# Twelve pairs of weight buffers shifted in 32-byte steps against the activations they are multiplied with

## The chip, the core and the metric

The kernel runs on one core of a Trainium2 chip. The metric is the device time of one execution in microseconds (us). The core's engines are called PE (TensorE's matrix multiplies), PEld (its weight loads, which run beside the multiplies), DVE (VectorE), ACT (ScalarE), POOL (GpSimd) and SP (SyncE, which issues the DMAs here).

## The reference

Linear attention with a feature map, then two multilayer perceptrons on its output:

```python
def phi(x):                                   # x: (4, 8, 576, 64), w_phi: (64, 128)
    proj = np.einsum('bhsd,df->bhsf', x, w_phi)
    proj = proj - np.max(np.abs(proj), axis=-1, keepdims=True)
    return np.concatenate([np.exp(proj), np.exp(-proj)], axis=-1)
q_p, k_p = phi(q), phi(k)
kv = np.einsum('bhsf,bhsd->bhfd', k_p, v);  z = np.sum(k_p, axis=2)
num = np.einsum('bhsf,bhfd->bhsd', q_p, kv)
den = np.einsum('bhsf,bhf->bhs', q_p, z)[..., None] + 1e-06
x = (num / den) as (2304 tokens, 512)
h = x @ w_in1;  x = (h * np.cos(h)) @ w_out1                            # 512 -> 2048 -> 512
h = x @ w_in2;  out = (max(h, 0) + alpha * min(h, 0)) @ w_out2          # 512 -> 2048 -> 512
```

The four weight matrices come in 8-byte floats; the kernel takes them as pairs of 32-bit words and decodes them on the chip.

## The kernel before

**Attention first.** Eight groups of four heads are worked off in chunks of tokens: projections (`pj`, line 455), the sums over keys (`kv`, line 496), transposes (`tp`, line 536) and the numerators (`nm`, line 580). The normalised result is written as two tiles, `xh` and `xl`, each 128 partitions x 4 x 2304 of type float32r. `xh` is the value rounded to float32r, `xl` is what is left over.

**Then the two perceptrons.** Every operand of these products is such a high and low pair, and `mm3` (line 160) makes each product of three multiplies: high by high, high by low, low by high. The hidden features are cut into 16 tiles of 128 per layer, the tokens into groups of 512, 512, 512, 512 and 256. A step is one feature tile for one token group: `hidden` makes four products, 12 multiplies into a PSUM tile `ph`, with the weights `wih`, `wil` stationary and `xh`, `xl` moving. `turns`, `gate` and `activate` make the activation and its pair `gh`, `gl` on ACT, DVE and POOL, some steps ahead. `output` makes again 12 multiplies (6 for the 256-token group in the second layer, where the tokens are the rows) into PSUM tiles `po`: in layer 1 with `woh`, `wol` stationary and `gh`, `gl` moving, in layer 2 the other way round. The Python code fixes the order of every engine's instructions; there is no planner behind it.

**The weight buffers.** `w_tile` (line 90) gives each decoded weight tile a buffer of 128 partitions x 512 float32r values, 2048 bytes in a partition. There are six slots (`WSLOTS`), each with a high and a low buffer for `w_in` (`wih0`, `wil0`, ...) and for `w_out` (`woh0`, `wol0`, ...), so twelve pairs. Slots 0 and 1 lie in `wpool`, slots 2 to 5 in `wpool2`, which is opened where the attention's buffers were. `w_instructions` (line 95) decodes a tile in ten instructions on ACT, DVE and POOL; `fetch_w` (line 138) starts its DMA.

**Where things lie.** In the built program, `xh`, `xl`, all five buffers each of `gh` and `gl`, and all 24 weight buffers start at a byte address that leaves 352 when it is divided by 512. (A tile of 128 bytes, `edge`, at the far end of the memory is used by nothing and shifts `gh` and `gl` there.) Every piece of 128 weight columns and every 512-token piece of x begins a multiple of 512 bytes further, so that in the perceptrons the stationary operand that is being loaded and the moving operand that is being streamed always lie at distance 0 modulo 512. In the attention's numerators they don't: the stationary tiles `kvh`, `kvl` start at 480, 32, 96 and 160 modulo 512, are read in pieces of 66 columns (264 bytes) at offsets that are multiples of 264, and the moving tiles `qp0h`, `qp0l`, `qp1h`, `qp1l` are read from 224 and 480.

Of the kernel before, what the change touches and what calls it, by code (L numbers as in the profile page):

```python
# [10 lines left out]
F32 = mybir.dt.float32  # L11
# [10 lines left out]
P = 128  # L22
# [6 lines left out]
def feature_map_attention_two_mlps(  # L29
# [52 lines left out]
    w_t = {}  # L82
    w_pools, w_temps = [wpool], [wtmp]
    staged, decoding = [], []

    def split(hi, lo, src, lo_engine):
        nc.scalar.copy(hi, src)  # L87
        lo_engine.tensor_tensor(out=lo, in0=src, in1=hi.bitcast(F32), op=ALU.subtract)  # L88

    def w_tile(slot, nm):  # L90
        s = slot % WSLOTS
        pool = w_pools[0 if s < WSLOTS_A else 1]
        return pool.tile([P, DM], F32R, tag=f"{nm}{s}", name=f"{nm}{s}")

    def w_instructions(spare=True):
# [15 lines left out]
        def to_hi():  # L111
            hl.extend(w_tile(layer * NFT + ft, f"w{'io'[which]}{x}") for x in "hl")
            w_t[layer, which, ft] = tuple(
                z.rearrange("p (k f) -> p k f", k=KD) if which == 0 else z for z in hl
            )
            copy(hl[0], tf)
# [683 lines left out]
```

## Time and profile before

| | |
|---|---|
| time, median of 2 runs | 987.65 us (987.52 to 987.78) |
| time of the profiled execution | 987.77 us |
| its span, from the first to the last instruction | 986.0 us |
| mean granted TensorE clock | 0.999 of 2.4 GHz |
| PE busy | 978.1 us (99%), 5145 multiplies |
| PEld busy | 838.0 us (85%) |
| DVE, ACT, POOL busy | 688.5, 493.9, 606.5 us |

The multiplies overlap one another in the records (one of 512 columns is shown as 390 ns long), so a busy PE says only that it never ran dry. How fast it goes is read from the distance between the starts of two multiplies that follow each other; below this is called a step.

### The profile page before, as it was taken

To read this page: it belongs to the slowest core of one execution; us is meant where nothing else is said; L and a number is where in the kernel's file an instruction comes from. 1 tells how busy PE (TensorE), PEld (TensorE's weight loads), DVE (VectorE), ACT (ScalarE), POOL (GpSimd) and SP (SyncE) were. 2 spreads that over 40 slices of the span, in tenths; PEclk is the share of its full clock that TensorE was granted. 3 is DMA by queue.
4 is the path that set the end of the run, shared out by engine and by line. 5 is a ranking of instruction groups with operands and counts; after the bars stand their busy time and mean duration, and the time that the engine had idled before them with its cause. 6 is when DMAs were issued, how large, how long until landed. Compare 5 with 4: busy or idle time off the path is not lost.

```text
span 986.0 us, 13997 instructions
## 1 busy us (share of the span) xinstructions
PE 978.1 (99%) x5145; PEld 838.0 (85%) x5145; DVE 688.5 (70%) x976; ACT 493.9 (50%) x967; POOL 606.5 (62%) x498
## 2 busy tenths in 40 slices
PE   8999999999999999999999999999999999999998
PEld 7999999888888888888888888888888888888886
DVE  6878687677987577747774788588748874885343
ACT  5888788867666467546755654132213221322110
POOL 3577777856666457535756789567636763676221
PEclk9999999999999999999999999999999999999999
DMA  6454544211121112101110112011101110110112
GB/s 164 113 140 126 142 114 115 66 52 51 57 65 44 43 43 65 44 22 43 64 44 22 44 43 65 22 43 65 43 22 44 65 43 23 43 64 1 43 59 91
DMA packets 64580, 60.63 MB, mean 61 GB/s; under 512 B 28928, under 2 KB 54656, under 8 KB 64512
## 3 DMA queue, kind: packets, MB, share of 16 engines
q1 hardware_dynamic: 64512, 59.75, 20.5%
q8 instruction: 40, 0.66, 0.3%
q14 instruction: 28, 0.23, 0.1%
HBM read 52.50 MB, written 4.79 MB: 58 GB/s over the span
## 4 chain that ended last, share of the span: by engine, by line
PE 94%; ACT 2%; DVE 1%; issue 1%; DMA 1%; POOL 1%; SPq 0%; POOLq 0%; ACTq 0%
PE po L165 39%; PE ph L165 38%; PE pj L455 6%; PE kv L496 5%; PE nm L580 5%; PE tp L536 2%; DMA acc<-in_q_dram 0%; DMA dn<-acc 0%; ACT acc L555 0%; DVE r L192 0%; DVE wt L127 0%; ACT acc L593 0%; ACT r L195 0%; ACT r L184 0%; ACT r L196 0%
## 5 line engine op out<-in xcount | busy, mean ns | idle before, releaser
L88 POOL TENSOR_TENSOR gl<-r,gh 128x512 fp32r<-128x512 f32 (+1 forms) x160 | 204.2, 1277 | 294.7 <-ACT gh L87 289.7
L87 ACT CAST gh<-r 128x512 fp32r<-128x512 f32 (+1 forms) x160 | 92.1, 576 | 382.5 <-DVE r L211 261.8
L165 PE MATMUL ph<-xl,wih 128*128 128x512 f32 (+1 forms) x640 | 235.7, 368 | 0.3 <-POOL xl L624 0.3
L165 PE MATMUL ph<-xh,wih 128*128 128x512 f32 (+1 forms) x640 | 235.5, 368 | 0.0
L165 PE MATMUL ph<-xh,wil 128*128 128x512 f32 (+1 forms) x640 | 235.4, 368 | 0.0
L245 DVE TENSOR_TENSOR acc<-po,acc 128x512 f32<-128x512 f32 (+1 forms) x134 | 86.1, 658 | 96.9 <-PE po L165 96.9
L165 PEld LDWEIGHTS ph<-xl,wih 128*128 128x128 f32 x640 | 120.6, 188 | 21.1 <-POOL xl L624 0.6
L165 PEld LDWEIGHTS ph<-xh,wih 128*128 128x128 f32 x640 | 120.6, 188 | 20.7
L165 PEld LDWEIGHTS ph<-xh,wil 128*128 128x128 f32 x640 | 120.5, 188 | 20.1
L165 PE MATMUL po<-gh,wol 128*128 128x512 f32 (+1 forms) x320 | 117.8, 368 | 0.2 <-POOL wol L135 0.2
L165 PE MATMUL po<-gl,woh 128*128 128x512 f32 (+1 forms) x320 | 117.9, 368 | 0.0
L165 PE MATMUL po<-gh,woh 128*128 128x512 f32 (+1 forms) x320 | 117.9, 368 | 0.0
L165 PE MATMUL po<-woh,gh 128*128 128x512 f32 x288 | 112.4, 390 | 0.0
L165 PE MATMUL po<-wol,gh 128*128 128x512 f32 x288 | 112.3, 390 | 0.0
L165 PE MATMUL po<-woh,gl 128*128 128x512 f32 x288 | 112.1, 389 | 0.1
L124 DVE SCALAR_TENSOR_TENSOR wt<-ws,we 128x512 int32<-128x512 int32 x64 | 98.4, 1537 | 2.4
L198 DVE TENSOR_SCALAR r<-ph,al 128x512 f32<-128x512 f32 (+1 forms) x80 | 55.3, 691 | 55.8 <-PE ph L165 35.6
L209 DVE TENSOR_TENSOR r<-ph,r 128x512 f32<-128x512 f32 (+1 forms) x80 | 50.5, 631 | 48.5 <-ACT r L196 48.3
L133 POOL TENSOR_TENSOR wu<-wu,we 128x512 f32<-128x512 f32 x64 | 82.9, 1295 | 1.3 <-ACT wu L130 1.3
L571 POOL TENSOR_TENSOR qp1l<-acc,qp1h 128x512 fp32r<-128x512 f32 (+1 forms) x64 | 59.2, 951 | 26.6 <-ACT qp1h L569 26.6
L496 PEld LDWEIGHTS kv<-vm,kp 128*128 128x128 f32 x512 | 72.5, 191 | 2.6 <-ACT qp1h L569 0.4
L496 PE MATMUL kv<-vm,kp 128*128 128x66 f32 x512 | 72.5, 255 | 0.1
(81 smaller groups left out, 1877.5 us busy)
## 6 DMA issues: line engine op xcount, KB each, us to landing
ws<-in_moe_w_in_dram SPq DMA_DIRECT2D x32, 512.0 KB, 3.7
ws<-in_moe_w_out_dram SPq DMA_DIRECT2D x32, 512.0 KB, 3.5
acc<-dr SPq DMA_DIRECT2D x32, 144.0 KB, 3.1
out_dram<-acc SPq DMA_DIRECT2D x18, 256.0 KB, 2.0
vm<-in_v_dram SPq DMA_DIRECT2D x16, 256.0 KB, 3.7
kin<-in_k_dram SPq DMA_DIRECT2D x28, 128.0 KB, 2.9
qin<-in_q_dram SPq DMA_DIRECT2D x28, 128.0 KB, 2.9
acc<-acc SPq DMA_DIRECT2D x16, 144.0 KB, 2.3
```

Of the source, the lines that this page charges most:

```text
L87: nc.scalar.copy(hi, src)
L88: lo_engine.tensor_tensor(out=lo, in0=src, in1=hi.bitcast(F32), op=ALU.subtract)
L124: lambda: stt(out=t, in0=w1, scalar=-0x40000000, in1=e, op0=ALU.bitwise_and, op1=ALU.bitwise_or),
L133: lambda: tt(out=u, in0=u, in1=ef, op=ALU.mult),
L165: nc.tensor.matmul(ps, lhsT=l, rhs=r, start=(first and m == 0), stop=(last and m == n - 1))
L198: nc.vector.tensor_scalar(out=r, in0=ph, scalar1=0.0, scalar2=al[:, ft:ft + 1], op0=ALU.min, op1=ALU.mult)
L209: nc.vector.tensor_tensor(out=r, in0=ph, in1=r, op=ALU.mult)
L245: nc.vector.tensor_tensor(out=a, in0=po, in1=a, op=ALU.add)
L455: nc.tensor.matmul(pj[:, a].rearrange("p j f -> p (j f)"), lhsT=x[:, a * P:(a + 1) * P], rhs=w2.rearrange("p j f -> p (j f)"), start=True, ...
L496: nc.tensor.matmul(ps[:, :, y, :] if pr is None else ps[:, pr, y, :], lhsT=e[:, s, 2 * a + y, :], rhs=vt[:, y] if pr is None else vm[:, pr ...
L571: nc.gpsimd.tensor_tensor(out=dl, in0=et, in1=dh.bitcast(F32), op=ALU.subtract)
L580: nc.tensor.matmul(nm, lhsT=l[:, s, pr, y * VW:(y + 1) * VW], rhs=r[:, s, y, :], start=(s == 0 and m == 0), stop=(s == 1 and m == 2),)
```

## The change

The first time that the high buffer of a pair is asked for, an unused tile of 128 partitions x 8 float32 values (32 bytes in a partition) is taken from the same pool just ahead of it:

```diff
+    skewed = set()
 ...
     def w_tile(slot, nm):
         s = slot % WSLOTS
         pool = w_pools[0 if s < WSLOTS_A else 1]
+        if nm[2] == "h" and (nm, s) not in skewed:
+            skewed.add((nm, s))
+            pool.tile([P, 8], F32, tag=f"{nm}{s}skew", name=f"skew{s}")
         return pool.tile([P, DM], F32R, tag=f"{nm}{s}", name=f"{nm}{s}")
```

In the built program the pairs then start at these distances behind x (and behind `gh`, `gl`, which stay where they were), modulo 512; high and low buffer of a pair have the same one:

| pair | slot 0 | slot 1 | slot 2 | slot 3 | slot 4 | slot 5 |
|---|---|---|---|---|---|---|
| `wih`, `wil` | 32 | 64 | 160 | 192 | 288 | 320 |
| `woh`, `wol` | 96 | 128 | 224 | 256 | 352 | 384 |

What is allocated behind them on the same side moves too: the accumulators `acc` and all of the attention's left-hand tiles (`qin`, `kvh`, `kvl`, `qp0h` and so on) by 128 bytes, the second set of decoding temporaries by 384. The tiles on the right (`kin`, `kp`, `vm`, `gh`, `gl`, `r`) do not move. The instructions of every engine, their order and their waits are the same as before, row by row; only line numbers and addresses differ.

## Rows read from the trace of the kernel before

**Rows 1.** The page's parts 1 and 4: busy engines, and the chain by line.

```profile
PE 978.1 (99%) x5145; PEld 838.0 (85%) x5145; DVE 688.5 (70%) x976; ACT 493.9 (50%) x967; POOL 606.5 (62%) x498
...
PE po L165 39%; PE ph L165 38%; PE pj L455 6%; PE kv L496 5%; PE nm L580 5%; PE tp L536 2%; DMA acc<-in_q_dram 0%; DMA dn<-acc 0%; ACT acc L555 0%; DVE r L192 0%; DVE wt L127 0%; ACT acc L593 0%; ACT r L195 0%; ACT r L184 0%; ACT r L196 0%
```

**Rows 2.** Whom PE waited for: total us, times, longest us.

```profile
PE tp L432 <- DVE half_pi L434: 1.5, 1, 1.5
PE pj L455 <- DMA acc<-in_q_dram: 1.2, 1, 1.2
PE tp L536 <- ACT qp0h L569: 0.4, 1, 0.4
PE ph L165 <- POOL xl L624: 0.3, 1, 0.3
PE po L165 <- POOL wol L135: 0.2, 1, 0.2
```

**Rows 3.** PE's groups by shape: count | busy us, mean ns | idle before.

```profile
L165 PE MATMUL ph<-xh,wih 128*128 128x512 f32 x512 | 199.5, 390 | 0.0
...
L165 PE MATMUL po<-woh,gh 128*128 128x512 f32 x288 | 112.4, 390 | 0.0
...
L165 PE MATMUL po<-gh,woh 128*128 128x512 f32 x256 | 99.8, 390 | 0.0
...
L165 PE MATMUL ph<-xh,wih 128*128 128x256 f32 x128 | 36.0, 282 | 0.0
...
L165 PE MATMUL po<-gh,woh 128*128 128x256 f32 x64 | 18.0, 282 | 0.0
```

**Rows 4.** Chain of work, 215 to 240 us: start us, us, what.

```profile
222.84 2.72 PE po L165 x12
225.56 2.72 PE ph L165 x12
```

**Rows 5.** Chain of work, 519 to 530 us: a 256-token group in layer 1.

```profile
523.53 1.43 PE ph L165 x12
524.96 2.75 PE po L165 x12
```

**Rows 6.** PE's timeline behind those 256-column multiplies: start us, shown length us.

```profile
524.80 0.40 PE L165 MATMUL po<-gh,woh 128*128 128x512 f32 x1
525.03 0.40 PE L165 MATMUL po<-gl,woh 128*128 128x512 f32 x1
525.27 0.39 PE L165 MATMUL po<-gh,wol 128*128 128x512 f32 x1
525.50 0.40 PE L165 MATMUL po<-gh,woh 128*128 128x512 f32 x1
525.73 0.39 PE L165 MATMUL po<-gl,woh 128*128 128x512 f32 x1
525.96 0.39 PE L165 MATMUL po<-gh,wol 128*128 128x512 f32 x1
```

**Rows 7.** PE's timeline at 39 us: numerators, `kvh` from 480 modulo 512.

```profile
39.55 0.31 PE L580 MATMUL nm<-qp1h,kvl 128*66 128x320 f32 x1
...
40.42 0.31 PE L580 MATMUL nm<-qp1h,kvl 128*66 128x320 f32 x1
```

**Rows 8.** PE's timeline at 62 us: the same, `kvh` from 32 modulo 512.

```profile
62.52 0.31 PE L580 MATMUL nm<-qp1h,kvl 128*66 128x320 f32 x1
...
63.41 0.32 PE L580 MATMUL nm<-qp1h,kvl 128*66 128x320 f32 x1
```

**Rows 9.** PE's timeline at 191 us: the last group's numerators, then layer 1.

```profile
191.45 0.28 PE L580 MATMUL nm<-qp0h,kvh 128*66 128x256 f32 x1
...
192.75 0.28 PE L580 MATMUL nm<-qp0h,kvl 128*66 128x256 f32 x1
192.87 0.40 PE L165 MATMUL ph<-xh,wih 128*128 128x512 f32 x1
```

**Rows 10.** PE's timeline at 151 us: float32 projections, two passes a multiply.

```profile
151.29 1.03 PE L455 MATMUL pj<-w,kin 128*128 128x256 f32 x4
152.15 0.59 PE L455 MATMUL pj<-w,qin 128*128 128x256 f32 x2
```

**Rows 11.** PEld's groups by shape: count | busy us, mean ns | idle before.

```profile
L165 PEld LDWEIGHTS ph<-xh,wih 128*128 128x128 f32 x640 | 120.6, 188 | 20.7
...
L580 PEld LDWEIGHTS nm<-qp1h,kvh 128*66 128x66 f32 x64 | 8.8, 138 | 0.7
```

## The prediction

> **What bounds the kernel now.** I read the page's busy engines and its chain by line first, then PE's waits, then PE's multiplies by shape, and last the chain and PE's timeline inside the perceptrons. The first two say that nothing but TensorE counts: PE is busy for 978.1 of 986.0 us, the chain lies on it for 94% by the sum of its lines, 77% in `ph` and `po` alone, and all of PE's shown waits together are 3.6 us [rows 1, 2]. DVE at 70%, POOL at 62% and ACT at 50% are cover enough: in the whole run PE waited once for a decoded weight, 0.2 us [rows 1, 2]. So the change can only count through the steps of the multiplies themselves, and through those that read a weight buffer.
>
> There are 3 x (512 + 288 + 256) = 3168 of them with 512 moving columns and 3 x (128 + 64) = 576 with 256 [rows 3]; each of these rows stands for three of one count, for high by high, high by low and low by high. Twelve of the large ones take 2.72 us, so a step is 226.7 ns; twelve of the small ones take 1.43 us, 119.2 ns [rows 4, 5]. The difference, 107.5 ns for 256 columns, is 0.42 ns a column, which is 2.4 GHz, the clock granted all along. What is left is a fixed cost: 226.7 - 512 x 0.417 = 13.3 ns for the large, 119.2 - 106.7 = 12.5 ns for the small. Over 3744 multiplies that is 3168 x 13.3 + 576 x 12.5 = 49 us of the run, and it is all that a change of addresses could win. All these multiplies have the weights at distance 0 modulo 512 from what they stream, so the perceptrons alone don't say whether the 13 ns hang on the distance.
>
> **What the change adds and removes.** No instruction is added, removed or moved and no wait changes, so the engines' work is the same, and the memory taken for the gaps, 384 bytes a partition, has no time. Three parts are left.
>
> First, the distance itself, in 3744 multiplies. The trace of before has one place where multiplies of the same type run at other distances: the numerators. Between the starts of the first and last of seven there are six steps. In a group whose `kvh` starts at 480, with distances from the weights being loaded to the operand being streamed of 24, 280, 408, 312, 312 and 440, they take 0.87 us, 145.0 ns a step [rows 7]; with 320 columns that leaves a fixed cost of 145.0 - 133.3 = 11.7 ns. In the next group `kvh` starts 64 bytes further on modulo 512, every distance is larger by 64, and the six steps take 0.89 us, 148.3 ns, a fixed cost of 15.0 ns [rows 8]. These two lists alternate over seven of the eight groups. In the last group eleven steps of 256 columns, at distances from 88 to 496, take 1.30 us, 118.2 ns each, or 11.5 ns over the columns [rows 9]. So the address does move a step, by some 3 ns between the two lists, but nowhere is the fixed cost gone, and the 13.3 ns of distance 0 lie in the middle of what the other distances show. Those loads are of 66 columns, not 128. The one step here in which a full 128-column `wih` is loaded at a distance, 128, while 256 columns stream, is 192.87 - 192.75 = 0.12 us [rows 9], no longer and no shorter than the 119.2 ns at distance 0.
>
> There is a reason why a load of 128 columns should care less than one of 66. A load takes 188 ns for 128 columns and 138 ns for 66 [rows 11], so 50 ns for 62 columns, 0.81 ns a column, against 0.417 ns for the moving operand. While 128 weight columns are read the moving read therefore gains about (0.81 / 0.417 - 1) x 128 = 120 columns on it, 480 of 512 bytes (an estimate from these rows): whatever the distance at its start, nearly every distance is passed once. A load of 66 columns passes half of them, and there the start matters.
>
> Bounds for the first part: if all 3744 multiplies had the fixed cost of the cheaper list, 11.7 ns, the gain would be 1.6 x 3744 = 6.0 us; with that of the dearer, 15.0 ns, the loss would be 1.7 x 3744 = 6.4 us. Twelve distances mix both, and their middle, 13.35 ns, is the 13.3 ns of before. I take 0.
>
> The Trainium skill has a rule against the change: the page "SBUF — State Buffer", section "Who interferes with whom", gives TensorE two read ports, one for the moving operand and one for the weight load, independent of each other, and says "PE and ACT never wait on anyone". By it the distance would be worth nothing and the time would stay at 987.8. The trace does not bear it out to the last nanosecond, since the two lists differ by 3.3 ns a step at the same shapes, but it does in size.
>
> Second, the attention's tiles on the left move by 128 bytes. `kvh`, `kvl` and the `qp` tiles move together, so the numerators keep their distances; the sums over keys read `kp` and `vm`, which stay. The projections of q get another distance to `w2`. They are float32 in two passes; four of them in a row, whose distance is different for k and q already, take 152.15 - 151.29 = 0.86 us, 215 ns for two passes over 256 columns, 213.3 ns by the clock [rows 10]: nothing there to win, and no sign of anything to lose. 0, with 2 us either way at most: `pj` is 6% of the span [rows 1], 59 us, half of it for q, and 2 us would be 7% of that half, more than the 3.3 ns in 145 between the lists.
>
> Third, decoding and activation: DVE, ACT and POOL read and write the shifted buffers and the shifted second set of temporaries. If some of that became slower it would be hidden while those engines have the idle third that the page shows; DVE is the fullest, and if that cover were gone the wait would be on a decoded weight, now 0.2 us in all [rows 1, 2]. 0.
>
> The sum: 987.77 (the profiled execution, 0.12 over the median of the runs shown, and 1.8 over its span) + 0 + 0 + 0 = 987.8 us, with 981 to 995 for this case.
>
> **The rivals.** *Slower: the two reads fall out of step.* At distance 0 the load and the stream have settled into a rhythm of 226.7 ns. That this is a rhythm and not a limit shows behind each group of 256-column multiplies: the first five steps of 512 columns take 525.96 - 524.80 = 1.16 us, 232.0 ns each, and only then is it 226.7 ns again [rows 6, 4], with the same addresses modulo 512 and nothing waited for. If at most other distances the rhythm is not found and the step stays at 232.0, the loss is 5.3 ns: 3168 x 5.3 = 17 us for the large ones, 20 us with the small ones, so 1004.6 to 1007.6. It decides as soon as more than about half of the twelve pairs settle there; with a quarter of them the result is inside my own range. For it: the row itself, and the 3.3 ns between the lists. Against it: the lists' middle, and the 0.12 us step.
>
> *Faster: the fixed cost is a collision of two reads.* At distance 0 both reads begin in the same place modulo 512; spread out, they might hardly meet. The float32 projections show how little a fixed cost can be: (215 - 213.3) = 1.7 ns [rows 10]. Going from 13.3 to 1.7 ns would win 11.6 x 3744 = 43 us: 944. Against it: at some twenty distances in the numerators the cost was 11.5 to 15.0 ns [rows 7 to 9], and the projections stream two passes in which the moving read is no faster per column than the load, and are of another type. If only half of it goes, it is 966.
>
> The Trainium skill's page "TensorE: Matmul & The Clock Gate", section "Back-to-back issue gap", gives N / 2.4 + 2.5 ns for a warm multiply, about 216 ns for 512 columns; by this the faster rival would be right and the run some 40 us shorter, if all that is above it here came from the distance. The same section adds that a real stream of load and multiply pairs is set by both.
>
> *The change does nothing of what it says.* It does: the built program has twelve distances, 32 to 384, so I give this no chance of its own.
>
> **How the numbers follow.** My forecast, no change beyond 981 to 995, has a chance of 0.75; the slower rival 0.16, the faster 0.09. A measurement of this kernel tells about 2% from no change, 19.8 us: 967.9 and 1007.4. The forecast lies wholly within. Of the slower rival most of the price, 1004.6 to 1007.6, is just within too, but a distance may settle worse than 232.0 ns (the first two steps behind the small ones are 0.23 and 0.24 us [rows 6]), so I put 0.09 above 1007.4. Of the faster one 0.07 lies below 967.9. That makes 0.07 faster, 0.84 same, 0.09 slower. The range of 8 in 10 is not symmetric: it runs from 980, the lower bound of the sum with the projections' 2 us, to 1006, most of the slower rival.
>
> **What would show it.** In the profile after, the chain's pieces of twelve multiplies should be 2.72 us within some 0.04 for all weight slots, and PE's waits the same five short ones. Pieces of 2.78 us for most pairs would show the slower rival, with the span growing by the pieces and by nothing else; pieces near 2.59 us (twelve of 216 ns) the faster one. Pieces that differ by slot, the same each time a slot comes round, would show that the distance matters and which is best. The projections and the numerators should take what they took. The prediction is wrong if a full load of 128 columns is more sensitive to its start than one of 66, against the estimate above, or if the distances are not equally good on the average and 0 was one of the best or worst.

## The result and the profile after

The changed kernel takes 1002.29 us (1001.97 to 1002.61), the one before 987.65: a ratio of 1.0144, with a 95% interval of 1.0128 to 1.0160. It became slower by 14.6 us. That lies inside the range of 980 to 1006 that I gave, but it is not what I forecast as likeliest, which was no change; it is most of the slower rival.

The page of the changed kernel, parts 1 and 4, to be held against [rows 1]:

```profile
span 1000.1 us, 13997 instructions
...
PE 992.9 (99%) x5145; PEld 837.6 (84%) x5145; DVE 685.6 (69%) x976; ACT 493.8 (49%) x967; POOL 606.9 (61%) x498
...
PE ph L169 40%; PE po L169 40%; PE pj L459 6%; PE kv L500 5%; PE nm L584 5%; PE tp L540 2%; DMA acc<-in_q_dram 0%; POOL qp1l L575 0%; ACT acc L559 0%; SPq L422 0%; ACT qp0h L573 0%; ACT acc L597 0%; ACT qp1h L573 0%; SPq L429 0%; POOLq L799 0%
```

The number of multiplies is the same and so is the time of every other engine, to within 3 us. PE alone is busy for 14.8 us more, and the chain gained it in `ph` and `po`. PE's waits (us, times, longest) are three of the five short ones of [rows 2] and no new one; those for `xl` and `wol` are gone:

```profile
PE tp L436 <- DVE half_pi L438: 1.5, 1, 1.5
PE pj L459 <- DMA acc<-in_q_dram: 1.1, 1, 1.1
PE tp L540 <- ACT qp0h L573: 0.4, 1, 0.4
```

So nothing waits for another engine; the steps themselves grew. The chain of the changed kernel, start us and length us, in the stretch that answers to [rows 4]:

```profile
222.39 2.79 PE po L169 x12
225.18 2.80 PE ph L169 x12
227.98 2.80 PE po L169 x12
230.78 2.80 PE ph L169 x12
233.58 2.80 PE po L169 x12
236.38 2.74 PE ph L169 x12
239.12 1.43 PE po L169 x12
```

and at 536 to 550 us, beside [rows 5]:

```profile
536.65 1.41 PE ph L169 x12
538.06 2.80 PE po L169 x12
540.86 2.79 PE ph L169 x12
543.65 2.72 PE po L169 x12
546.37 2.80 PE ph L169 x12
549.17 1.40 PE po L169 x12
```

Twelve multiplies of 512 columns take 2.80 us, 233.3 ns a step, where they took 2.72 us, 226.7 ns. Two pieces stand out. The one at 236.38 us, 2.74, reads `wih3`, at distance 192. The one at 543.65 us, 2.72, reads `woh3`, at distance 256: the old step, in the middle of the slower ones. The multiplies of 256 columns did not become slower but a little faster, 1.40 or 1.41 us for twelve against 1.43.

Taken over the starts of all multiplies in the trace, the 512-column steps sum up to 736.5 us (720.4 before, so 16.1 more) and the 256-column ones to 67.8 us (69.4, so 1.6 less; 0.5 of this is one long step in which PE waited for `xl` before, so the steps themselves gained about 1 us). The first multiply of the perceptrons starts 0.4 us earlier. 16.1 - 1.6 - 0.4 = 14.1 us, by which the span grew. So nearly the whole change is in the steps of the multiplies that read weight buffers.

The same starts, sorted by slot, show each distance by itself (512 columns, means within the hidden products of layer 1 and within its output products): 233.7 ns at 32, 233.4 at 64, 233.9 at 96, 233.1 at 128, 233.2 at 160 and 224, 229.1 at 192, 228.9 at 256 (the median is 227), and 233.2, 233.4, 233.9 and 232.5 at 288, 320, 352 and 384.

### The profile page after: what moved, and what is told of

Same layout as the page of the kernel before. It is cut to its first block, busy times and chain, and to the rows that moved or that the text cites. A ratio compares the mean times of both kernels' runs of the same rounds, so it can differ in the third digit from the quotient of the medians.

```text
span 1000.1 us, 13997 instructions
## 1 busy us (share of the span) xinstructions
PE 992.9 (99%) x5145; PEld 837.6 (84%) x5145; DVE 685.6 (69%) x976; ACT 493.8 (49%) x967; POOL 606.9 (61%) x498
## 4 chain that ended last, share of the span: by engine, by line
PE 97%; ACT 1%; issue 1%; DMA 0%; SPq 0%; POOL 0%; DVE 0%; POOLq 0%; ACTq 0%
PE ph L169 40%; PE po L169 40%; PE pj L459 6%; PE kv L500 5%; PE nm L584 5%; PE tp L540 2%; DMA acc<-in_q_dram 0%; POOL qp1l L575 0%; ACT acc L559 0%; SPq L422 0%; ACT qp0h L573 0%; ACT acc L597 0%; ACT qp1h L573 0%; SPq L429 0%; POOLq L799 0%
## 5 line engine op out<-in xcount | busy, mean ns | idle before, releaser
L169 PE MATMUL ph<-xl,wih 128*128 128x512 f32 (+1 forms) x640 | 238.2, 372 | 0.0
L169 PE MATMUL ph<-xh,wil 128*128 128x512 f32 (+1 forms) x640 | 238.0, 372 | 0.0
L169 PE MATMUL ph<-xh,wih 128*128 128x512 f32 (+1 forms) x640 | 238.0, 372 | 0.0
```

The source lines that it names most:

```text
L169: nc.tensor.matmul(ps, lhsT=l, rhs=r, start=(first and m == 0), stop=(last and m == n - 1))
```

## The experiments

The theory after this result: the step is set by the distance, modulo a power of two, between the weights that are being loaded and the operand that is streamed meanwhile; 0 and 256 are good, most others cost about 6 ns per multiply of 512 columns. Three rivals: **A**, the absolute place of the weights counts; **B**, it is not the distance but its change from one tile to the next that spoils the rhythm (in the changed kernel every twelve multiplies have another distance); **C**, a multiply is slowed by where its own weights lie, not by the load beside it. Where an edit is given it is against the kernel before, except that `gap_512` and `low_32` are against the change.

**rigid_32.** Everything moves by 32 bytes together.

```diff
-    edge.tile([P, 32], F32, name="edge")
+    edge.tile([P, 24], F32, name="edge")
     const = ctx.enter_context(tc.tile_pool(name="const", bufs=1))
+    const.tile([P, 8], F32, name="shift")
```

Expected: 

> The kernel before, with x, gh, gl, all weight buffers and everything else moved together by 32 bytes, so that every distance stays 0 modulo 512 and every absolute address changes. Theory (the distance between the weights being loaded and the operand being streamed, modulo 512, sets the step): no change, 987.7 us, steps of 226.7 ns. Rival A (the absolute place of the weight buffers counts, 352 modulo 512 being a good one): about as slow as the change, 1000 to 1005 us. Rival B (a step depends on how the distance changes from one tile to the next, since the rhythm is disturbed by each change): 987.7 us.

Measured: 987.77 us, ratio 0.9999 (0.9988 to 1.0011). Rival A falls: the weights start at 384 modulo 512 in place of 352, and nothing happens as long as x, `gh` and `gl` go along. In the next run the weights start at the same 384 and x stays at 352.

**all_32.** One gap in front of all weight buffers, one distance for all pairs.

```diff
     wpool = ctx.enter_context(tc.tile_pool(name="wpool", bufs=1))
+    wpool.tile([P, 8], F32, name="shift")
```

Expected: 

> One gap of 32 bytes in front of the first weight buffer alone, so that all twelve pairs lie at the same distance 32 from x, gh and gl. Theory (distance): steps of 512 columns stay near the 233 ns that the changed kernel shows at 32, so 1002 to 1006 us. Rival A (absolute place of the weights): slower as well, 1000 to 1005 us, since they start at 384. Rival B (changes of distance disturb the rhythm): all distances are equal, the rhythm settles, 988 us.

Measured: 1005.25 us, ratio 1.0170 (1.0141 to 1.0200). Rival B falls: with one distance throughout the kernel is slower than with twelve. Its chain in the stretch of [rows 4]:

```profile
222.52 2.80 PE po L166 x12
225.32 2.80 PE ph L166 x12
228.12 2.80 PE po L166 x12
230.92 2.80 PE ph L166 x12
```

The rhythm does settle, but at 233.3 ns.

**all_256.** The same edit with 64 values (256 bytes) in place of 8.

Expected: 

> One gap of 256 bytes in front of the first weight buffer alone: all pairs at distance 256. Theory, in the form that two distances are good, 0 and 256 (in the changed kernel the output tiles at 256 come down to 227 ns after some eight steps): 987 to 990 us. Theory, in the form that only 0 is good: 1002 to 1006 us. Rival A: slow, 1000 to 1005 us. Rival B: 988 us.

Measured: 987.58 us, ratio 0.9999 (0.9987 to 1.0010). Its chain, behind a group of 256-column multiplies:

```profile
218.13 2.75 PE po L166 x12
220.88 2.72 PE ph L166 x12
223.59 2.72 PE po L166 x12
```

2.75 once and then 2.72, as in [rows 4, 5]. A distance of 256 bytes is as good as none: the period is 256, not the 512 of the change's description. The changed kernel agrees, where distances 256 apart have steps within 0.6 ns of each other (32 and 288, 64 and 320, 96 and 352, 128 and 384).

**gap_512.** The change itself with gaps of 512 bytes.

```diff
-            pool.tile([P, 8], F32, tag=f"{nm}{s}skew", name=f"skew{s}")
+            pool.tile([P, 128], F32, tag=f"{nm}{s}skew", name=f"skew{s}")
```

Expected: 

> The change with gaps of 512 bytes in place of 32: as many gaps in the same places, but all distances 0 modulo 512 again. Theory (distance modulo 512): 987.7 us. If the gaps themselves or the moved accumulators and temporaries cost the time, or if the period is longer than 512 bytes: 995 to 1003 us.

Measured: 987.83 us, ratio 0.9998 (0.9987 to 1.0010). The gaps themselves cost nothing, and a period longer than 512 is excluded. What lies behind the gaps moves by multiples of 512 here, not by the 128 and 384 bytes of the change, so of those shifts this run says nothing.

**low_32.** High buffers at distance 0, low buffers at 32: a gap of 8 values ahead of each low buffer and of 120 values ahead of each high one but the first.

```diff
-        if nm[2] == "h" and (nm, s) not in skewed:
+        if (nm, s) not in skewed:
+            gap = 8 if nm[2] == "l" else 120 if skewed else 0
             skewed.add((nm, s))
-            pool.tile([P, 8], F32, tag=f"{nm}{s}skew", name=f"skew{s}")
+            if gap:
+                pool.tile([P, gap], F32, tag=f"{nm}{s}skew", name=f"skew{s}")
```

Expected: 

> All high buffers at distance 0 modulo 512, all low buffers at distance 32 (gaps of 32 bytes in front of each low buffer, 480 in front of each high one). In a product of three the order of the loads is high, high, low, and each load runs while the multiply before its own streams. Theory (the distance between the weights being loaded and the operand streaming beside it): in the hidden products the multiply of xl, beside which the low weights are loaded, gets the longer steps, 231 to 235 ns, the other two stay near 227; about a third of the loss of uniform 32, 6 us, so 993 to 995 us. Rival C (a multiply is slowed by its own weights' place): the multiply of xh by the low weights gets the longer steps, the same total. If the rhythm is what counts and one load in three out of place spoils it for all: steps of 231 to 235 in all three, 1000 to 1005 us.

Measured: 1005.77 and 1009.09 us, ratio 1.0194 (1.0145 to 1.0243). Part of the slower time, that of the profiled execution, lies in the attention: PE waited 2.2 us for a DMA there, the granted clock was then 0.5 (1.2 GHz) from 11 to 18 us, and the first hidden product began 3.6 us later than before. In its total this is the third of the outcomes named: the 512-column steps sum up to 739.5 us, as in `all_32` (739.1), so one load in three out of place costs as much as all three. PE's timeline, start us and shown length us:

```profile
223.49 0.40 PE L171 MATMUL ph<-xh,wih 128*128 128x512 f32 x1
223.72 0.40 PE L171 MATMUL ph<-xl,wih 128*128 128x512 f32 x1
223.96 0.39 PE L171 MATMUL ph<-xh,wil 128*128 128x512 f32 x1
224.19 0.40 PE L171 MATMUL ph<-xh,wih 128*128 128x512 f32 x1
```

Three multiplies take 224.19 - 223.49 = 0.70 us, 233 ns each on average, as in `all_32`. By the starts of all 512-column hidden multiplies the means are 232.6 ns for `xh` by `wih`, 239.1 for `xl` by `wih`, and 228.5 for `xh` by `wil`. The longest is the one beside which the low weights are loaded, and the shortest the one that uses them: rival C falls. But my expectation of a third of the loss was wrong, and so was an even 231 to 235 ns in all three. The two multiplies with a load in place beside them are longer than 226.7 ns as well, most of all the one that comes two steps behind the load out of place: the disturbance goes on into the steps after it.

**x_16 and x_8.** x is moved up by 16 or 8 bytes, all else stays where it was modulo 512.

```diff
-    xh = xpool.tile([P, KD, NTOK], F32R, name="xh")
+    xh = xpool.tile([P, KD * NTOK + 128], F32R, name="xh")[:, 4:4 + KD * NTOK]
+    xh = xh.rearrange("p (k n) -> p k n", k=KD)
 (the same for xl; x_8 starts at 2)
```

Expected for 16: 

> x (xh and xl) moved up by 16 bytes against everything else, so that the 1920 multiplies of the hidden products run at distance -16 and the output products at 0. Theory, if the good distance is exactly a multiple of 256: hidden steps near 233 ns, 1536 x 6 = 9 us, 996 to 998 us. Theory, if the load and the stream can slip against each other by a few columns and settle in the good rhythm from nearby: 988 us. If a distance between 0 and 32 is better than 0: under 986 us.

Expected for 8: 

> The same with 8 bytes, distance -8 for the hidden products. Theory, exact multiple of 256: 996 to 998 us. Theory, settling from nearby: 988 us, at 8 bytes more surely than at 16. If a distance between 0 and 32 is better than 0: under 986 us.

Measured: 996.47 us, ratio 1.0083 (1.0054 to 1.0112), and 1000.48 us, ratio 1.0124 (1.0094 to 1.0153). Two pieces of the chain of each, first x_16, then x_8:

```profile
219.77 2.78 PE ph L167 x12
222.54 2.75 PE po L167 x12
```

```profile
220.16 2.81 PE ph L167 x12
222.97 2.75 PE po L167 x12
```

Eight bytes, two columns, are enough: hidden steps of 231.7 ns at -16 and 234.2 ns at -8. Nothing settles from nearby. The output products, still at distance 0, take 2.75 in place of 2.72 us each time, because they start out of rhythm behind the hidden ones, as they do behind 256-column multiplies in [rows 5, 6]. With 8 bytes under x the hidden 512-column steps sum up to 10.7 us more than before and the output ones to 2.2 us more, together about the 12.8 us by which the kernel is slower; 9 had been the price for the hidden ones alone at 233 ns. With 16 bytes it is 7.0 and 2.6 us.

**all_128 and all_192.** The edit of `all_32` with 32 and 48 values.

Expected for 128: 

> All twelve pairs at distance 128. Theory, period 256 bytes with only its multiples good: steps near 233 ns as at 32, 1003 to 1006 us. Rival, period 128 (0, 32 and 256 tried alone can't tell it from 256): 988 us.

Expected for 192: 

> All twelve pairs at distance 192, so the weights 192 behind x, gh and gl in the hidden products and layer 1, and 64 short of a multiple of 256. In the changed kernel the hidden steps at 192 were 229 ns, those at other distances 233. Theory, each distance has its own settled step: hidden steps 229 ns, the layer 2 output at -192, that is 64 modulo 256, near 232 ns: 994 to 998 us. Theory, all but multiples of 256 are equal: 1003 to 1006 us.

Measured: 1005.14 us, ratio 1.0167 (1.0138 to 1.0197), and 998.01 us, ratio 1.0095 (1.0066 to 1.0124). One piece of the chain of each, first 128, then 192:

```profile
225.15 2.80 PE ph L166 x12
```

```profile
225.54 2.75 PE ph L166 x12
```

128 is no period; half of 256 is as bad as 32. 192 has a settled step of its own, 229.2 ns, between the two. So the step depends on the distance in more than two grades, and the fast one belongs to multiples of 256 alone among those tried.

**half and half_32.** The hidden products load 64 weight columns, and the upper half of each tile of hidden features is left out from there on; `half_32` adds the gap of `all_32`.

```diff
-        ph = pools["ps_h"].tile([P, 512], F32, tag="ph", name="ph")[:, 0:n]
+        ph = pools["ps_h"].tile([P, 512], F32, tag="ph", name="ph")[0:64, 0:n]
-            ((wh[:, kk, :], wl[:, kk, :]), (xh[:, kk, c0:c0 + n], xl[:, kk, c0:c0 + n]))
+            ((wh[:, kk, 0:64], wl[:, kk, 0:64]), (xh[:, kk, c0:c0 + n], xl[:, kk, c0:c0 + n]))
 ... (r, gh, gl, al, half_pi and the output weights likewise cut to 64 partitions)
```

Expected for distance 0: 

> Left out: hidden features 64 to 127 of each tile, from the hidden products on to the output products, so that the hidden products load 64 weight columns in place of 128 and stream the same 512 columns of x; the output products load 128 columns of 64 rows. All distances 0 as in the kernel before. Theory, in the form that the 13.3 ns over the columns are reads of the load that get in the way of the stream, one by one: with half of the load half of them, hidden steps of 220 ns, 1536 x 6.7 + 384 x 6 = 12.6 us less, 975 us. Rival D (a fixed cost of each pair of load and multiply, whatever the length of the load): 226.7 ns, 987.7 us. Output steps 227 ns in both.

Expected for distance 32: 

> The same left out, with all weight pairs at distance 32. Theory, collisions one by one: hidden steps of 223 ns (half of the 20 ns over the columns that uniform 32 showed), output steps 233 ns, 990 us. Rival D: hidden and output steps at 233 ns as in uniform 32, 1005 us. If the distance matters only when a load is long enough to pass a whole period: hidden steps of 227 ns at 32 as well, about 996 us.

Measured: 1046.88 us, ratio 1.0593 (1.0562 to 1.0624), and 1055.39 us, ratio 1.0679 (1.0648 to 1.0710). The total tells nothing on the question, since these kernels pay for something else (last section). The steps do. PE's timeline of `half` within one hidden product, then of `half_32`:

```profile
226.54 0.39 PE L165 MATMUL ph<-xl,wih 128*64 128x512 f32 x1
...
228.85 0.39 PE L165 MATMUL ph<-xh,wil 128*64 128x512 f32 x1
```

```profile
226.96 0.39 PE L166 MATMUL ph<-xl,wih 128*64 128x512 f32 x1
...
229.28 0.40 PE L166 MATMUL ph<-xh,wil 128*64 128x512 f32 x1
```

Ten steps take 2.31 us, 231 ns each, at distance 0, and 2.32 us, 232 ns, at 32; over all hidden products, without their first and last steps, the means are 230.6 and 231.8. Neither the 220 ns of collisions counted one by one nor the 226.7 ns of rival D came out. With a load of 64 columns distance 0 is not good any more, and of the two distances tried 0 is better by some 1 ns only.

The output products of the same two kernels still load 128 columns, of 64 rows. The four steps between the 8th and the 12th start of one such product, on PE's timeline of `half` and then of `half_32`:

```profile
225.04 0.39 PE L165 MATMUL po<-gl,woh 64*128 64x512 f32 x1
...
225.95 0.39 PE L165 MATMUL po<-gh,wol 64*128 64x512 f32 x1
```

```profile
225.42 0.39 PE L166 MATMUL po<-gl,woh 64*128 64x512 f32 x1
...
226.36 0.39 PE L166 MATMUL po<-gh,wol 64*128 64x512 f32 x1
```

0.91 us is 227.5 ns a step at distance 0, 0.94 us is 235 ns at 32. So with 128 columns loaded the effect is there, on half of the rows too, and at distance 0 some seven steps behind the change of shape are enough to come back to the fast step. The hidden products, of twelve multiplies as well, don't come back. Whether a longer run of 64-column loads would find a faster rhythm stays open.

**tail_64.** In the changed kernel, 256-column multiplies at 64 had been shorter than at 0. So everything stays as before, but the 256-token group of x and of layer 1's `gh` and `gl` moves up by 192 bytes, which puts the weights at -192, that is 64 modulo 256, from it.

```diff
+    TAIL, OFF = groups[-1][0], 48
+    def xcols(c0, n):
+        return slice(c0 + OFF, c0 + OFF + n) if c0 >= TAIL else slice(c0, c0 + n)
-    xh = xpool.tile([P, KD, NTOK], F32R, name="xh")
+    xh = xpool.tile([P, KD, NTOK + 64], F32R, name="xh")
-            ((wh[:, kk, :], wl[:, kk, :]), (xh[:, kk, c0:c0 + n], xl[:, kk, c0:c0 + n]))
+            ((wh[:, kk, :], wl[:, kk, :]), (xh[:, kk, xcols(c0, n)], xl[:, kk, xcols(c0, n)]))
+        o = OFF if layer == 0 and n < 512 else 0
+        gh, gl = gh[:, o:o + n], gl[:, o:o + n]
 ... (xl likewise; the writes of x cut in two where they cross into the last group)
```

Expected: 

> The kernel before, with the 256-token group of x and of layer 1's gh and gl moved up by 192 bytes, so that the weights lie at distance 64 modulo 256 behind it; all multiplies of 512 columns stay at a multiple of 256. In the changed kernel 256-column multiplies at distance 64 had steps of 113 to 116 ns where distance 0 has 120. Theory (the distance alone sets the settled step, and for 256 columns 64 is better than 0): 576 multiplies at 113.3 to 116.2 ns, 2.2 to 3.9 us less, 984 to 985.5 us, if the first 512-column steps behind them lose no more than before. If those lose more than that (they need some five steps to settle, 48 times): 988 us or more. Cost of the eight instructions added in the attention, which split a write in two: hidden.

Measured: 984.82 us (984.47 to 985.57) beside 988.0, ratio 0.9967 (0.9955 to 0.9979): faster than both kernels. Its chain in the stretch of [rows 5]:

```profile
522.93 1.41 PE ph L169 x12
524.34 2.72 PE po L169 x12
527.06 1.41 PE ph L169 x12
```

The 256-column step went from 119.5 to 117.9 ns by the starts of all of them, less than the 113 to 116 I had hoped for. The rest of the gain I had set down as a risk: the 512-column products behind them now take 2.72 us, not 2.75. The smaller products leave the rhythm intact for those that follow. 576 x 1.6 ns = 0.9 us and 48 x 0.03 us = 1.4 us make 2.3 us. The span of the profiled execution shrank by 2.4 us (986.0 to 983.6), though PE waited 0.6 us longer for `xl` in it; the medians are 3.2 us apart, and the rest of that is not accounted for.

## Why the prediction was right and wrong

**The range held by way of a rival.** 1002.29 us lies above the 981 to 995 of my own sum. It lies under 1006 only because I had drawn the range up to there for the slower rival, so the hit says nothing for the mechanism that I believed in.

**What bounds the kernel** held. Nearly all of the change is in the steps of multiplies that read weight buffers, and no new wait took a part. Here the steps were read the right way, by the distance of starts: PE's busy share was 99% before and after.

**The step that failed is the first part of the sum, "I take 0".** I took the fixed cost at distances other than 0 from the numerators [rows 7 to 9], found 13.3 ns in the middle of their 11.5 to 15.0, and concluded that twelve distances cost what one does. That neighbour was wrong in two ways. It loads 66 columns, and `half` and `half_32` show 231 and 232 ns with 64: neither 0 nor 32 is a good distance for so short a load, so there was nothing to lose. And it streams 320 or 256 columns, while the loss shows at 512 and not at 256: in the changed kernel 256-column steps became shorter on average. (A full load beside 320 columns was not run.) At 512 columns the cost over the columns is 13.3 ns at multiples of 256 and 233.3 - 213.3 = 20 ns at 32 and at 128.

The 3.3 ns between the two lists, which I read as the work of the distance, are not that alone. In the changed kernel the numerators keep their distances, and the six steps of [rows 8] take 63.41 - 62.54 = 0.87 us there, as in the other list, not 0.89:

```profile
62.54 0.31 PE L584 MATMUL nm<-qp1h,kvl 128*66 128x320 f32 x1
...
63.41 0.31 PE L584 MATMUL nm<-qp1h,kvl 128*66 128x320 f32 x1
```

In `all_256` the same list takes 0.87 us in the group at 62 us and 0.89 us in the one at 108 us. What else sets them is not shown.

**The estimate that a 128-column load passes every distance** and so should not care where it starts was sound arithmetic from [rows 11] with a wrong conclusion. `all_32`, `all_128` and `x_8` show that the start does decide, down to two columns. The one step of 0.12 us that seemed to confirm it [rows 9] had 256 columns beside it, where the effect is absent.

**The slower rival was right, and from the right rows.** The first steps behind 256-column multiplies, 232.0 ns [rows 6], were almost the only place of the old trace where 512-column multiplies ran out of their rhythm, and the changed kernel's 512-column steps have a mean of 736.5 / 3167 = 232.6 ns. Its price was 17 us for the large ones, and 16.1 came out. That the two numbers are so near is in part luck: 232.0 is the mean of five steps on the way back to the fast rhythm, while the steps at 32 or 128 stay at 233.3 for good. It also charged the small ones with 3 us, and they gained about 1. I gave it 0.16. The row that spoke for it had the shape of the multiplies in question, the rows against it had another; weighing them by that would have given it more. "It decides as soon as more than about half of the twelve pairs settle there" was borne out: of the 512-column multiplies only those at 256, and in part at 192, kept near the old step.

**The second and third parts held** within what they allowed. The attention, whose left-hand tiles moved by 128 bytes, reached the first hidden product 0.4 us earlier. That is not the projections but the numerators, which I had said would take what they took: up to there their steps sum up to 0.4 us less. Decoding and activation cost PE no new wait.

**The faster rival** has no run for it: at none of the distances tried, the change's twelve among them, did twelve 512-column multiplies take less than 2.72 us, and no single step was under 223 ns. The 216 ns that follow from the Trainium skill's formula for a warm multiply taken by itself ("TensorE: Matmul & The Clock Gate", section "Back-to-back issue gap") appeared in no run here. And the Trainium skill's rule ("SBUF — State Buffer", section "Who interferes with whom") that TensorE's two read ports are independent does not agree with these runs: the same instructions with nothing to wait for took 17.5 us more when one operand was moved by 32 bytes (`all_32`). The measurement decides.

What exactly the two reads share is not shown. Shown are the operand that matters (the load beside the stream, by the order of the steps in `low_32`), the period (256: 0, 256 and 512 are equal; -8, -16, 32, 128 and 192 are not), and that a loss came with loads of 128 columns beside streams of 512, and not beside streams of 256.

## What to carry to other kernels

Where a kernel is bound by back-to-back float32r multiplies of 512 columns with a weight load beside each, let stationary and moving tiles start at the same byte address modulo 256; here the other distances tried cost 1 to 3% of the step, with no wait anywhere in the profile to show it. (The 256-column multiplies were better off at 64 than at 0, by 1.6 ns a step and by what they spared the products behind them.) Read such a kernel by the distance between starts, in pieces of equal multiplies, since the busy share stays at 99% either way. And when the trace of before has to stand in for an operation that it doesn't show, take the row with the same shape under odd conditions, not the row with the right conditions and another shape.

## What the runs showed that I had not expected

A multiply's step carries a memory. After 256-column multiplies, or after products at another distance, some five or six steps at a good distance are 5 ns too long on average before the fast rhythm is back ([rows 6], and 2.75 against 2.72 us in `x_16` and `x_8`). In `low_32` one load in three out of place costs as much as all three.

A change of the array's shape costs far more. In `half` each switch between hidden products (128 rows by 64 columns) and output products (64 rows by 128 columns) stops the overlap of load and stream. Both kernels change the rows and the columns of the array at once, so which of them does it is not shown. The last output multiply and the first hidden ones on PE's timeline, and the first hidden loads on PEld's:

```profile
225.95 0.39 PE L165 MATMUL po<-gh,wol 64*128 64x512 f32 x1
226.26 0.44 PE L165 MATMUL ph<-xh,wih 128*64 128x512 f32 x1
226.54 0.39 PE L165 MATMUL ph<-xl,wih 128*64 128x512 f32 x1
```

```profile
226.26 0.13 PEld L165 LDWEIGHTS ph<-xh,wih 128*64 128x64 f32 x1 [0.35 <-issue]
226.31 0.14 PEld L165 LDWEIGHTS ph<-xl,wih 128*64 128x64 f32 x1
226.54 0.13 PEld L165 LDWEIGHTS ph<-xh,wil 128*64 128x64 f32 x1
```

The first load of the new shape starts 0.31 us after the start of the multiply before it, not beside it, and the two steps around it are 0.31 and 0.28 us, where 0.23 is usual. On the way back from hidden to output products it is alike. The first and last steps of all products come to some 53 us more than usual, of the 59 us by which the span grew (986.0 to 1045.0): loading half of the columns made the kernel slower.
